# Batch 0's convolutions issued behind the score reductions of heads 6 to 8, and the conv weights loaded first by ScalarE's queue

## The chip, the cores and the metric

The kernel runs on one core of a Trainium2 chip. The metric is the device time of one execution in microseconds; the kernel before has a median of 501.28 us in 3 runs (501.0 to 501.86).

## What is computed

Four batches of eight attention heads (sequence 576, head size 64) are followed by a gated layer and by a gated layer with spatial mixing. Cut to what matters:

```python
cum = np.cumsum(np.maximum(s, 0.0), axis=-1)
scores = q @ k.T / 8 + np.minimum(-(cum[:, None] - cum[None, :]), 0.0)   # per head, causal
x = softmax(scores) @ v                      # heads laid side by side: 4 x 576 x 512
gate = sigmoid(sum(conv_w[k] * x_padded[:, k:k + S] for k in range(5)))  # causal, per channel
y = gate * (x @ w_val) @ w_out
h = np.maximum(y @ w_in, 0.0)                # 1024 wide: u, v
v_n = (v - mean(v)) / np.sqrt(var(v) + 1e-6)
out = (u * (w_spatial @ v_n + b_spatial)) @ w_out2
```

## The kernel before

A head's scores are made in five row tiles (64 rows and four of 128). TensorE writes them to two PSUM banks; VectorE's reduction in L253 adds the mask and takes the extreme of a row, then a read of one column puts it into `nm`; ScalarE makes the exponentials (L258), and their sums stand in `sm`. The function `transposes` turns the probabilities on TensorE (`pst`) and copies them on ScalarE (L301, tile `pt`). For each pair of heads `pv` multiplies them with v (`pso`, `psq`), and VectorE multiplies with the divisors R, which come back by DMA in a broadcast form, and writes x (L326 to L329). The first eight heads' scores are products of raw float32 data (L242); from head 8 on q and k are split on VectorE into a high and a low part (L100, `qk`, `kd`) and two products are summed (L244, L245). Wherever a weight is multiplied, `three` makes three products of high and low parts.

`conv(b, p)` is the convolution of one pair of heads (128 channels): ScalarE's scaling by the last tap (L338), four VectorE steps on 128x575, 574, 573 and 572 elements (L341), ScalarE's Tanh (L343). It needs x of the pair and `cw`, the conv weights.

The weights come as 64-bit floats. `from_f64` loads one (L402), unpacks it on ScalarE (L404), VectorE (L405 to L407) and GpSimd (L410, L411) into 32 bits; `fold_prep` and `weight_prep` then split it. `first_steps` does so for the conv weights, w_out (`wo_h`, `wo_l`), one half of w_in (`wih`, `wil`) and w_val, and then makes four folds, products of w_in and w_out (`psm` in the rows below, 12 products each); the result is `wch`, `wcl`.

The main loop over `w` issues scores of head w, transposes of head w - 1 and `pv` and `conv` of an earlier pair. In between, `more(n)` lets the weight steps and, from w = 9 on, the mixing layers (generators in `queue`) go on by a quota. A scheduler that simulates the program's time sets each engine's order; `tc.issue_after(X)` keeps what is issued in it behind X on X's own engine. `paced` uses it to keep the first weight steps behind `LAST["V"]`, the latest reduction issued. With `chain[0]`, from w = 18 to 31, TensorE keeps the order in which the code issues its work; this is so both in the kernel before and in the changed one.

## Time and profile before

| | |
|---|---|
| median of 3 runs | 501.28 us |
| the profiled execution's own time | 502.31 us |
| its span, first to last instruction | 500.5 us |
| mean granted clock of TensorE | 0.993 of full speed |
| TensorE busy with products | 474.9 us |
| VectorE busy | 320.2 us |
| ScalarE busy | 315.4 us |
| GpSimd busy | 165.8 us |

The rows further down are of this one execution. PE is TensorE, DVE VectorE, ACT ScalarE, POOL GpSimd, SPq the DMA issues of SyncE. Times are microseconds from the span's start. A line such as L341 is that of the kernel before; L75 and L100 are helpers which many steps share, so there the tiles tell the steps apart. A busy share is a mean over stages which different engines set, so the stretches are read one by one.

### The profile page before, as it was taken

The page shows a single profiled execution, that of the slowest core. Times are in us where ns is not written, and L with a number is a line of the kernel's source. Part 1 is how long each engine was busy: PE and PEld are TensorE (multiplying, and loading weights), DVE is VectorE, ACT ScalarE, POOL GpSimd, SP SyncE. Part 2 cuts the span into 40 slices and gives each one's busy share as a digit, 9 for nine tenths or more (in the row PEclk, how much of TensorE's full clock was granted, in tenths as well). Part 3 has the DMA queues.
Part 4 walks back from the last instruction along what each step waited for, and adds up shares of the span by engine and source line. Part 5 has one row for each costly group of instructions (what it writes and reads, how often), then busy time and mean ns, then how long its engine had stood idle before and what let it go on. Part 6 is the DMA issues. An engine that isn't in the chain of part 4 may idle for free.

```text
span 500.5 us, 9139 instructions
## 1 busy us (share of the span) xinstructions
PE 474.9 (95%) x3138; PEld 400.7 (80%) x3138; DVE 320.2 (64%) x835; ACT 315.4 (63%) x796; POOL 165.8 (33%) x183
## 2 busy tenths in 40 slices
PE   8697789979999999999999999999999999999997
PEld 5453457768777898998879999888778989988997
DVE  5599999698989885655578476555794453124120
ACT  2787968786776876675577758674876624234322
POOL 5587452045583103103243023012342022136130
PEclk9898999999999999999999999999999999999999
DMA  3876477558383644287531412784510072600002
GB/s 93 223 250 209 108 256 252 158 158 236 118 265 113 182 128 123 76 252 231 145 88 43 130 47 80 230 249 129 168 42 28 0 279 54 211 1 2 0 13 84
DMA packets 51567, 68.23 MB, mean 136 GB/s; under 512 B 23936, under 2 KB 39456, under 8 KB 51520
## 3 DMA queue, kind: packets, MB, share of 16 engines
q1 hardware_dynamic: 46592, 62.84, 42.3%
q10 hardware_dynamic: 4928, 4.80, 2.9%
q8 instruction: 25, 0.41, 0.4%
q14 instruction: 22, 0.18, 0.1%
HBM read 54.91 MB, written 9.16 MB: 128 GB/s over the span
## 4 chain that ended last, share of the span: by engine, by line
PE 63%; DVE 20%; DMA 7%; ACT 3%; issue 3%; POOL 2%; SPq 1%; DVEq 0%; ACTq 0%; POOLq 0%
PE psm L75 45%; PE pso L75 5%; PE pst L75 5%; DVE p L253 4%; DVE z L341 3%; DMA wv<-wv_d 2%; PE pss L244 2%; DMA raw<-in_qk 2%; PE pss L245 2%; DVE v L583 2%; PE psw L75 1%; DVE qk L100 1%; DVE wg L407 1%; ACT p L258 1%; PE pss L242 1%
## 5 line engine op out<-in xcount | busy, mean ns | idle before, releaser
L258 ACT ACTIVATE p<-p,nm 64x64 f32<-64x64 f32 (+4 forms) x160 | 88.5, 554 | 22.6 <-DVE nm L253 22.2
L253 DVE CUSTOM_DVE_ANT_0 p<-pss,mask 64x64 f32<-64x64 f32 (+4 forms) x160 | 62.7, 412 | 25.1 <-PE pss L245 17.7
L301 ACT ACTIVATE pt<-pst 128x512 f32<-128x512 f32 (+2 forms) x128 | 59.0, 495 | 28.3 <-PE pst L75 28.1
L341 DVE SCALAR_TENSOR_TENSOR z<-x,cw,z 128x575 f32<-128x575 f32 (+1 forms) x64 | 57.3, 896 | 7.4 <-ACT z L338 7.1
L75 PE MATMUL pst<-ident,p 128*128 128x128 f32 x416 | 60.1, 276 | 2.0 <-ACT p L258 1.8
L100 POOL TENSOR_TENSOR y<-gt,y 128x288 fp32r<-128x288 f32 x32 | 27.1, 847 | 102.8 <-ACT y L93 102.8
L100 POOL TENSOR_TENSOR g<-gt,g 128x288 fp32r<-128x288 f32 x32 | 28.8, 903 | 95.0 <-ACT g L93 94.7
L75 PEld LDWEIGHTS pst<-ident,p 128*128 128x128 f32 x416 | 48.4, 141 | 11.2 <-ACT p L258 4.3
L75 PE MATMUL psm<-g,wch 128*128 128x288 f32 x256 | 55.1, 299 | 1.2 <-DVE wcl L100 0.9
L75 PE MATMUL pso<-pt,vraw 128*64 128x512 f32 (+4 forms) x320 | 52.1, 448 | 0.0
L75 PE MATMUL psm<-wch,g 128*128 128x512 f32 x144 | 47.7, 400 | 0.0
L244 PE MATMUL pss<-qk 128*64 128x64 f32 (+1 forms) x144 | 43.6, 320 | 2.7 <-DVE nm L253 2.3
L75 PEld LDWEIGHTS psm<-g,wch 128*128 128x128 f32 x256 | 42.4, 189 | 2.0 <-DVE wcl L100 1.2
L75 PE MATMUL psm<-y,wv 128*128 128x288 f32 x288 | 42.0, 297 | 0.5 <-ACT ot L629 0.5
L75 PE MATMUL psm<-xvh,wv 128*128 128x288 f32 x192 | 40.2, 300 | 1.7 <-DMA wv<-wv_d 1.3
L245 PE MATMUL pss<-kd,cn 66*64 66x64 f32 (+1 forms) x144 | 41.1, 294 | 0.0
L242 PE MATMUL pss<-raw 128*128 128x320 f32 (+4 forms) x96 | 31.5, 432 | 9.6 <-DVE nm L253 6.0
L75 PEld LDWEIGHTS psm<-y,wv 128*128 128x128 f32 x288 | 39.6, 188 | 0.9 <-ACT ot L629 0.7
L524 DVE TENSOR_TENSOR gt<-psm,u 128x288 f32<-128x288 f32 x32 | 14.5, 456 | 39.3 <-PE psm L75 31.2
L75 PEld LDWEIGHTS pso<-pt,vraw 128*64 128x64 f32 (+1 forms) x320 | 19.3, 138 | 23.4 <-issue 16.7
L75 PE MATMUL psm<-wsh,vh 128*128 128x288 f32 x128 | 38.0, 299 | 0.0
L75 PE MATMUL psm<-g,wcl 128*128 128x288 f32 x128 | 38.0, 297 | 0.0
(142 smaller groups left out, 1118.9 us busy)
## 6 DMA issues: line engine op xcount, KB each, us to landing
raw<-in_qk SPq DMA_DIRECT2D x24, 448.0 KB
wv<-wo_d SPq DMA_DIRECT2D x12, 512.0 KB
R<-r_d SPq DMA_DIRECT2D x32, 160.0 KB
wv<-wv_d SPq DMA_DIRECT2D x10, 512.0 KB
out<-ot ACTq DMA_DIRECT2D x32, 144.0 KB
vraw<-in_vp SPq DMA_DIRECT2D x32, 128.0 KB
cn<-qk SPq DMA_DIRECT2D x24, 144.0 KB
raw<-in_qk SPq DMA_DIRECT2D x48, 64.0 KB
```

The source lines that it names most:

```text
L75: m = op(*a, **k)
L100: eng.tensor_tensor(out=out_, in0=in_, in1=f(hi), op=ALU.subtract)
L242: nc.tensor.matmul(pst[0:m, o:o + b - a], r[:, 1, q0:q0 + m], r[:, 0, k0 + a:k0 + b], start=True, stop=True)
L244: nc.tensor.matmul(pst[0:m, o:o + b - a], qa[:, q0:q0 + m], kb[:, k0 + a:k0 + b], start=True, stop=False)
L245: nc.tensor.matmul(pst[0:m, o:o + b - a], qc[0:KD, q0:q0 + m], kd[0:KD, k0 + a:k0 + b], start=False, stop=True)
L253: LAST["V"] = V.tensor_tensor_reduce(out=row[:, a:b], in0=src, in1=mask[0:m, o:o + b - a], scale=-0.125, scalar=3.0e38 if a == 0 else nm[0 ...
L258: A.activation(row, row, AF.Exp, bias=nm[0:m, i:i + 1], scale=-1.0, accum_out=sm[h // 2 % 2][0:m, h % 2, i:i + 1])
L301: A.activation(PT[h][:, to:to + n], pt[:, o:o + n], AF.Copy)
L341: V.scalar_tensor_tensor(out=z[:, d:], in0=x[:, :S - d], scalar=cw[:, p, k:k + 1], in1=z[:, d:], op0=ALU.mult, op1=ALU.add)
L407: V.scalar_tensor_tensor(out=up, in0=a.bitcast(I32), scalar=3, in1=up, op0=ALU.logical_shift_left, op1=ALU.bitwise_or)
L524: V.tensor_tensor(out=t, in0=psrc, in1=other, op=ALU.mult)
L583: V.tensor_scalar(out=v[0:m], in0=v[0:m], scalar1=mv[0:m, 0:1], scalar2=rs[0:m], op0=ALU.subtract, op1=ALU.mult)
```

## The change

`from_f64` issues loads of fewer than 512 columns, which are the conv weights alone, on ScalarE's queue and the others on SyncE's as before. The conv weights are prepared right after the function's definition, ahead of all other weights and of `first_steps`. In the main loop, batch 0's convolutions leave their place behind `pv` at w = 2, 4, 6 and 8: pair 0 is issued behind the scores of head 6, pair 1 behind those of head 7, pairs 2 and 3 behind those of head 8, each behind the latest reduction. The last batch's last convolution stays at w = 32.

```diff
-        SY.dma_start(r, src.rearrange("p (c t) -> p c t", t=2))
+        (A if n < 512 else SY).dma_start(r, src.rearrange("p (c t) -> p c t", t=2))
...
+    cw = early.tile([128, NP, 5], F32, name="cw")
+    V.tensor_copy(cw, from_f64(conv_w, 20).rearrange("p (c k) -> p c k", k=5))
...
     def first_steps():
-        nonlocal cw
-        cw = early.tile([128, NP, 5], F32, name="cw")
-        V.tensor_copy(cw, from_f64(conv_w, 20).rearrange("p (c k) -> p c k", k=5))
...
+    LATER = {6: [0], 7: [1], 8: [2, 3]}
     prep(0)
     for w in range(NH + 1):
         chain[0] = 18 <= w < 32
...
         if w % 2 == 0 and (0 < w <= H or w == NH):
             pv(w - 2)
-            conv((w - 2) // H, ((w - 2) % H) // 2)
+            if w == NH:
+                conv(B - 1, NP - 1)
+        for p in LATER.get(w, []):
+            with tc.issue_after(LAST["V"].ins):
+                conv(0, p)
```

VectorE around the scores of head 4, before (`p_125` are the probabilities of even heads, `x_381` is x of pair 0, `z` the convolution's output):

```order
L268 RECIPROCAL rin<-den 128x10
L341 SCALAR_TENSOR_TENSOR z<-x_381,cw,z 128x575
L253 ISA p_125,nm<-pss,mask 128x448
L253 ISA nm 128x1
L100 TENSOR_TENSOR xvl_973<-x_381,xvh_972 128x576
L253 ISA p_125,nm<-pss,mask 128x256
L253 ISA nm 128x1
L341 SCALAR_TENSOR_TENSOR z<-x_381,cw,z 128x574
L100 TENSOR_TENSOR wil<-wg,wih 128x512
L341 SCALAR_TENSOR_TENSOR z<-x_381,cw,z 128x573
L253 ISA p_125,nm<-pss,mask,nm 128x320
```

The same place now:

```order
L268 RECIPROCAL rin<-den 128x10
L253 ISA p_125,nm<-pss,mask 128x448
L253 ISA nm 128x1
L100 TENSOR_TENSOR xvl_973<-x_381,xvh_972 128x576
L253 ISA p_125,nm<-pss,mask 128x256
L253 ISA nm 128x1
L253 ISA p_125,nm<-pss,mask,nm 128x320
```

The three conv steps have left this place, and one split of w_in that stood ahead of the last reduction stands behind it.

VectorE around the scores of head 7 (`p_128`, odd heads; `qk` and `kd_117` are the splits of head 8), before:

```order
L253 ISA p_128,nm<-pss,mask 128x448
L253 ISA nm 128x1
L100 TENSOR_TENSOR qk<-raw_66,qk 64x576
L407 SCALAR_TENSOR_TENSOR wg<-wg 128x512
L100 TENSOR_TENSOR kd_117<-raw_66,qk 64x576
L326 TENSOR_TENSOR x_724<-pso,R 128x384
L328 TENSOR_TENSOR x_724<-pso,R 128x128
L329 TENSOR_TENSOR x_724<-psq,R 128x64
L253 ISA p_128,nm<-pss,mask 128x256
L253 ISA nm 128x1
```

and now:

```order
L341 SCALAR_TENSOR_TENSOR z<-x_381,cw,z 128x574
L253 ISA p_128,nm<-pss,mask 128x448
L253 ISA nm 128x1
L407 SCALAR_TENSOR_TENSOR wg<-wg 128x512
L100 TENSOR_TENSOR wv<-wg,wv 128x512
L341 SCALAR_TENSOR_TENSOR z<-x_381,cw,z 128x573
L100 TENSOR_TENSOR qk<-raw_66,qk 64x576
L100 TENSOR_TENSOR kd_117<-raw_66,qk 64x576
L253 ISA p_128,nm<-pss,mask 128x256
L253 ISA nm 128x1
```

Two of pair 0's conv steps now stand ahead of head 7's 256-column reduction, and the x of pair 2 (`x_724`) has left the place ahead of it.

TensorE from head 7's 448-column product (`raw_67`) to head 8's first products (`qk`, `kd_117`), before; the rows left out are more fold products:

```order
L242 MATMUL pss<-raw_67 128x448
L75 MATMUL psm<-wih,wo_h 128x512
...
L75 MATMUL psm<-wil,wo_h 128x512
L242 MATMUL pss<-raw_67 128x256
L242 MATMUL pss<-raw_67 128x320
L75 MATMUL psm<-wih,wo_h 128x512
...
L75 MATMUL psm<-wil,wo_h 128x512
L244 MATMUL pss<-qk 64x64
L245 MATMUL pss<-kd_117,cn_115 64x64
L244 MATMUL pss<-qk 128x192
```

and now, from head 7's 256-column product on:

```order
L242 MATMUL pss<-raw_67 128x256
...
L75 MATMUL pst<-ident,p_125 128x128 x2
L242 MATMUL pss<-raw_67 128x320
L244 MATMUL pss<-qk 64x64
L75 MATMUL psm<-wih,wo_h 128x512
...
L75 MATMUL psm<-wil,wo_h 128x512
L245 MATMUL pss<-kd_117,cn_115 64x64
L244 MATMUL pss<-qk 128x192
```

Before, one fold stands ahead of head 7's last two products and one ahead of head 8. Now both stand, one behind the other, between the two products of head 8's first tile.

## Rows read from the trace of the kernel before

**Rows 1.** The page's first part: engine, busy time (share of the span), instructions.

```profile
PE 474.9 (95%) x3138; PEld 400.7 (80%) x3138; DVE 320.2 (64%) x835; ACT 315.4 (63%) x796; POOL 165.8 (33%) x183
```

**Rows 2.** Busy time by stretch: length, PE, PEld, DVE, ACT, POOL, clock, DMA, GB/s.

```profile
40.00:88.00 48.00, 40.52 (x203) 24.69 (x202) 47.07 (x122) 37.58 (x97) 23.68 (x16) 0.96 0.65 206
88.00:100.00 12.00, 12.00 (x81) 8.82 (x79) 7.22 (x22) 9.24 (x23) 0.00 (x0) 1.00 0.57 164
100.00:126.00 26.00, 23.03 (x164) 19.43 (x163) 24.14 (x63) 19.94 (x50) 13.99 (x12) 1.00 0.67 196
126.00:160.00 34.00, 32.89 (x173) 25.43 (x172) 32.05 (x75) 24.56 (x58) 21.19 (x21) 1.00 0.53 167
```

**Rows 3.** The chain of waits in order of time: start, length, work.

```profile
85.02 3.02 PE psm L75 x12
...
422.69 74.71 PE psm L75 x516
```

**Rows 4.** VectorE's timeline, 88 to 102: start, length, work, idle time ahead, its releaser.

```profile
91.91 0.22 DVE L253 CUSTOM_DVE_ANT_0 p<-pss,mask 64x64 f32<-64x64 f32 x1 [0.33 <-PE pss L245]
...
94.23 0.49 DVE L253 CUSTOM_DVE_ANT_0 p<-pss,mask 128x320 f32<-128x320 f32 x1 [1.82 <-PE pss L245]
...
96.50 0.69 DVE L100 TENSOR_TENSOR wil<-wa,wih 128x512 fp32r<-128x512 f32 x1 [1.77 <-PE pst L75]
...
99.48 0.56 DVE L326 TENSOR_TENSOR x<-pso,R 128x384 f32<-128x384 f32 x1 [0.81 <-DMA R<-r_d]
...
100.95 0.55 DVE L253 CUSTOM_DVE_ANT_0 p<-pss,mask,nm 128x320 f32<-128x320 f32 x1
```

**Rows 5.** The timeline of the start, all engines.

```profile
11.54 0.42 SPq L402 DMA_DIRECT2D wg<-in_conv_w  x1
...
12.01 0.45 SPq L402 DMA_DIRECT2D wg<-in_woT  x1
...
13.56 0.18 DVE L405 TENSOR_SCALAR wg<-wg 128x20 f32<-128x20 f32 x1 [1.42 <-ACT wg L404]
...
21.38 1.39 PE L242 MATMUL pss<-raw 128*64 128x64 f32 x4 [3.41 <-DMA raw<-in_qk]
```

**Rows 6.** Conv steps of L341 by stretch: length, busy (count), clock, DMA share, GB/s.

```profile
40.00:68.00 28.00, 7.25 (x8) 0.94 0.56 180
...
76.00:100.00 24.00, 3.23 (x4) 1.00 0.67 205
```

**Rows 7.** The timeline around heads 7 to 9, VectorE and TensorE.

```profile
71.76 0.35 DVE L253 CUSTOM_DVE_ANT_0 p<-pss,mask 128x192 f32<-128x192 f32 x1
...
79.59 0.19 PE L244 MATMUL pss<-qk 128*64 128x64 f32 x1
...
99.54 0.30 PE L244 MATMUL pss<-qk 128*128 128x320 f32 x1
```

**Rows 8.** TensorE's timeline, probabilities times v.

```profile
30.18 2.20 PE L75 MATMUL pso<-pt,vraw 128*64 128x512 f32 x16
...
44.70 3.84 PE L75 MATMUL pso<-pt,vraw 128*64 128x512 f32 x16
```

**Rows 9.** Busy time in the 4 us ahead and in those of the second product.

```profile
40.00:44.00 4.00, 2.32 (x10) 0.99 (x8) 4.00 (x14) 3.46 (x10) 2.26 (x2) 1.00 0.70 238
44.00:48.00 4.00, 3.51 (x13) 1.24 (x13) 4.00 (x10) 3.16 (x9) 3.46 (x2) 0.62 0.72 236
```

**Rows 10.** The timeline of GpSimd and VectorE around two conv steps.

```profile
58.15 1.04 POOL L411 TENSOR_TENSOR wa<-wr 128x512 int32<-128x512 int32 x1 [3.07 <-DVE nm L253]
...
58.60 1.20 DVE L341 SCALAR_TENSOR_TENSOR z<-x,cw,z 128x575 f32<-128x575 f32 x1
...
61.48 0.80 DVE L341 SCALAR_TENSOR_TENSOR z<-x,cw,z 128x574 f32<-128x574 f32 x1
```

**Rows 11.** VectorE's timeline, the first split of head 8.

```profile
75.78 0.76 DVE L100 TENSOR_TENSOR qk<-raw,qk 64x576 fp32r<-64x576 f32 x1
```

More of the change, by code (lines that the diff above doesn't have):

```diff
@@ L634, in tile_stickbreak_attention_moe @@
     queue = []
-    cw = None
     def more(n):
```

## The prediction

> **What bounds the kernel now.** I read the busy line of the page first: TensorE 474.9 us of a span of 500.5, VectorE 320.2 [rows 1]. That is an average over stages, so the second view is busy time by stretch [rows 2]. In it TensorE idles 7.48 us between 40 and 88 us (48 less 40.52), nothing between 88 and 100, 2.97 between 100 and 126 and 1.11 between 126 and 160. VectorE is the mirror image: it idles 0.93 us in 40 to 88, 4.78 in 88 to 100 and 1.86 in 100 to 126. So VectorE sets the pace of heads 4 to 7, TensorE that of heads 8 and 9 with their folds, VectorE again that of heads 10 and 11. The chain of waits ends in one TensorE piece of 74.71 us [rows 3]: late in the kernel the end moves only by what TensorE no longer loses early on. From head 23 on the two orders of TensorE are the same row for row.
>
> The four waits that make up VectorE's idle time after 88 us are 0.33, 1.82, 1.77 and 0.81 us; the first three end on TensorE, the last on the DMA of the divisors R for pair 3 [rows 4]. There is room there for VectorE work, and no room for it between 40 and 88.
>
> **The conv weights, first and by ScalarE's queue.** Three small VectorE steps, about 0.18 us each, now stand between the load of s and the end of the running sum: 3 x 0.18 = 0.54 us later for the sum and the row of it that head 0 needs [rows 5]. SyncE's list loses one issue, which held it from 11.54 to 12.01: 0.47 us sooner for what stands behind, the load of head 2 among it. VectorE's wait of 1.42 us for ScalarE's step on these weights goes, but TensorE then still waits 3.41 us for head 2's load until 21.38, so what head 1 gains ends there. The load of head 2 moves by 0.54 - 0.47 = 0.07 us. I take 0, between 0.5 lost (the delay reaches head 0's first product whole) and 0.5 gained (only the SyncE issue counts). ScalarE's table load now stands behind one DMA issue and has no one waiting for it until the running sum is done.
>
> **The convolutions of batch 0.** Before, the eight VectorE steps of pairs 0 and 1 take 7.25 us between 40 and 68, in the stretch that VectorE paces; pair 2's four take 3.23 us between 76 and 100 [rows 6]. Now pair 0's stand behind head 6, pair 1's behind head 7, pairs 2 and 3 behind head 8. The tie to the last reduction binds VectorE to its own order, so no other engine waits for a new semaphore; ScalarE's first conv step stays where it was in its list, its Tanh moves back with VectorE's steps, and what reads the gate is far behind. Nothing is added or dropped: at the last reduction of head 11 both VectorE lists have done the same work. The gain can therefore be no more than VectorE idle time, and after 40 us that is 0.93 + 4.78 + 1.86 = 7.57 us.
>
> Step one, to head 8. In the new TensorE order both folds (12 products each) stand behind head 8's first product, and that needs the PSUM bank which head 7's 256-column reduction frees. Up to that reduction the new VectorE list holds, against the old list up to head 7's 192-column reduction, five conv steps fewer (5 x 0.91 = 4.5 us, 0.91 being 7.25 / 8) and in their place three reductions, the two splits of head 8 and one more weight step, about 4.2 us. So it is reached 0.3 us before the old row's end at 72.1, at 71.8. Two folds at 3.02 us [rows 3] are done at 77.9. Before, they and head 7 were done at 79.6, where head 8's first product stood [rows 7]: 1.7 us gained.
>
> Step two, to the end of head 9. TensorE has 19.9 us of rows from there to head 9's last product at 99.54 [rows 7]; the new list holds no more, so it is there by about 97.6. Its reduction then ends some 0.6 us later, at 98.2, where it ended at 101.5 before [rows 4], because the wait for R and two weight steps no longer stand ahead of it: 3.3 us gained. TensorE by itself shows less, 99.54 - 97.6 = 1.9, so I hold 1.9 as the lower end.
>
> Step three, heads 10 and 11, paced by VectorE. The new list is 1.2 us shorter at head 9's end (one conv step and one weight step fewer) and equal at head 11's, so 1.2 us of the 3.3 is paid back. Of the 1.86 us that VectorE idled here I take half as filled, 0.9 (bounds 0 and 1.86). Sum: 3.3 - 1.2 + 0.9 = 3.0 us. From there TensorE paces and the gain reaches the end.
>
> What could lie in between: with the conv steps late, the x tiles are kept longer; x of pair 0 is next written at head 11, far behind. SyncE's list now loads head 6 ahead of two of the four w_val loads, so no head waits longer for its data. The product of probabilities and v for heads 2 and 3 cost 3.84 us where the same 16 products for heads 0 and 1 cost 2.20 [rows 8]: the granted clock was 0.62 there, after four us in which TensorE was busy 2.32 [rows 9]. TensorE's order up to there is unchanged, so I leave that loss of 1.64 us in (0 gained; 1.64 if the clock stays up).
>
> The profiled run took 502.31 us, so the sum gives 502.31 - 3.0 = 499.3 for it; that run stands 1.03 above the median of 501.28, so against the median it is **498.3 us**. The likeliest case's own range is 496.5 to 500.0 (4.8 gained if all idle time of 88 to 100 is refilled; 1.3 if step two gives only 1.9, step three pays back 1.2 and 0.6 of the idle time is filled).
>
> **Rivals.** *Cheaper conv steps.* A conv step that meets a GpSimd row takes longer: 1.20 us at 58.60 with GpSimd busy from 58.15 to 59.19, 0.80 us at 61.48 without [rows 10]. GpSimd is idle from 88 to 100 [rows 2]. If the eight moved steps all fall to 0.80, that is 7.25 - 6.40 = 0.85 us more: 497.4. For it: pair 2's four steps, 3.23 us, were already there. Against it: most new places lie before 88, where GpSimd still works. [...]
>
> *Head 8 late (slower).* Head 8's first product now has 24 fold products queued behind it on TensorE. It needs head 8's data, whose split was done on VectorE at 75.78 + 0.76 = 76.54 [rows 11]. Before, the folds ran meanwhile. If that split comes no sooner than it did, the folds end at 76.54 + 6.04 = 82.6, 3.0 us later than 79.6, and less the 1.2 us by which VectorE's list is shorter at head 9's end the time is 501.28 + 3.0 - 1.2 = 503.1. It decides against me once head 8's first product starts later than 79.6 - 6.0 = 73.6 us. Against it: the load is released by head 6's last product, and VectorE's list up to head 6's end is shorter by the eight conv steps alone by 7.25 us.
>
> *Given back later.* Between heads 9 and 22 the lists of TensorE and VectorE differ too, and one more wait of 1 us there or two costs what VectorE gained: TensorE lost 1.11 us in 126 to 160 already. With 2.7 us lost, 501.0. This is also where I put the case that waits for loads, not VectorE, pace heads 4 to 7 (SyncE's list moves less than VectorE's).
>
> **How the numbers follow.** Forecast 0.60, cheaper steps 0.10, given back 0.14, head 8 late 0.16. The first two are faster: 0.70; the third is same: 0.14; the fourth slower: 0.16. About 0.2% (1.0 us) is what a measurement of this kernel can tell from no change. For 8 in 10 the range runs from 496.0, with some 0.07 below it (all bounds on the good side), to 502.6, with some 0.11 of the slow case above it.
>
> **What would show it.** Right: VectorE full from 40 us on with its idle time of 88 to 100 us mostly gone; head 8's first product at 71 to 73 us; head 9's last reduction ending near 98; TensorE's idle time in 40 to 88 down from 7.5 to about 5.5 us; the piece that ends the chain as long as before and 3 us sooner. Wrong: head 8's first product after 73.6 with TensorE idle ahead of it; head 0's first product more than 0.5 us later; the gain there at 100 us and gone by 230.

## The result, and the profile after

| | before | after |
|---|---|---|
| median | 501.19 us (500.02 to 501.86, 6 runs) | 506.29 us (504.63 to 509.93, 6 runs) |
| the profiled execution's own time | 502.31 us | 505.85 us |
| its span | 500.5 us | 504.1 us |
| mean granted clock of TensorE | 0.993 | 0.983 |

The ratio is 1.010 (95% interval 1.0064 to 1.0137): the changed kernel is about 5 us slower, where 3 us faster was forecast. The two profiled executions, from which the rows come, are 3.5 us apart (505.85 less 502.31), so they show some 70% of it. Helper lines keep their numbers; L506, L522, L575 and L583 of before are L509, L525, L578 and L586 now.

The busy line of the page of after (us, share of the span, instructions), to be read against [rows 1]:

```profile
PE 479.0 (95%) x3138; PEld 403.9 (80%) x3138; DVE 324.8 (64%) x835; ACT 315.5 (63%) x796; POOL 164.2 (33%) x183
```

The counts of instructions are the same. TensorE is busy 4.1 us longer (474.9 before) and idle 25.1 us, 0.5 less than before (504.1 less 479.0; 500.5 less 474.9). The mean granted clock is lower too (0.983 against 0.993), so the first question is where the clock was low. Busy time by stretch of after (columns: PE, PEld, DVE, ACT, POOL with counts, granted clock, DMA share, GB/s), against [rows 2]:

```profile
40.00:88.00 48.00, 41.78 (x219) 24.96 (x218) 44.95 (x118) 38.53 (x98) 23.71 (x16) 0.96 0.70 218
88.00:100.00 12.00, 9.96 (x60) 7.83 (x60) 10.33 (x31) 9.59 (x24) 0.00 (x0) 0.99 0.47 124
100.00:126.00 26.00, 25.71 (x172) 22.27 (x172) 25.11 (x59) 19.83 (x51) 13.68 (x13) 0.94 0.63 196
126.00:160.00 34.00, 31.74 (x160) 24.20 (x159) 30.36 (x70) 22.93 (x56) 18.87 (x20) 0.95 0.50 164
```

VectorE's idle time of 88 to 100 us fell from 4.78 to 1.67 us, as meant; that of 40 to 88 rose from 0.93 to 3.05. TensorE's idle time of 126 to 160 rose from 1.11 to 2.26 us, and the clock there is 0.95. TensorE's waits from 90 to 232 us, summed by what was waited for (us in total, times, longest), first before, then after:

```profile
PE pss L244 <- DVE nm L253: 1.9, 2, 1.2
PE psr L75 <- DVE rin L268: 1.0, 1, 1.0
PE psm L75 <- DMA wv<-wv_d: 1.0, 1, 1.0
PE psm L75 <- DVE wcl L100: 0.9, 1, 0.9
PE pst L75 <- ACT p L258: 0.7, 1, 0.7
PE psm L75 <- DVE gt L522: 0.4, 1, 0.4
```

```profile
PE psm L75 <- DMA wv<-wo_d: 2.2, 1, 2.2
PE psr L75 <- DVE rin L268: 2.1, 1, 2.1
PE psm L75 <- DVE wcl L100: 1.3, 1, 1.3
PE pss L244 <- DVE nm L253: 0.8, 2, 0.6
PE psm L75 <- DVE gt L525: 0.3, 1, 0.3
```

The sums differ by 0.8 us only (5.9 and 6.7; TensorE's whole idle time there is 5.96 and 7.02). But the longest wait of before is 1.2 us, and after has two of over two. What follows them differs. Rows of TensorE's timeline of after (start, us, engine, line, operation, tiles, and in brackets the idle time ahead with what ended it):

```profile
72.89 0.21 PE L244 MATMUL pss<-qk 128*64 128x64 f32 x1 [1.93 <-DVE nm L253]
...
96.51 0.39 PE L244 MATMUL pss<-qk 128*128 128x320 f32 x1
...
98.98 0.54 PE L75 MATMUL psm<-xvh,wv 128*128 128x288 f32 x2 [1.33 <-DVE wcl L100]
...
131.78 0.27 PE L75 MATMUL psr<-ident,rin 128*10 128x128 f32 x1 [2.14 <-DVE rin L268]
...
219.36 4.90 PE L75 MATMUL psm<-y,wv 128*128 128x288 f32 x24 [2.19 <-DMA wv<-wo_d]
```

Behind three of these pauses the granted clock goes to half (0.50 of full speed). Windows of 2 us of after, same columns as the stretches above:

```profile
100.00:102.00 2.00, 2.00 (x10) 2.00 (x10) 1.97 (x3) 2.00 (x5) 0.00 (x0) 0.50 0.17 36
...
134.00:136.00 2.00, 2.00 (x6) 1.51 (x5) 2.00 (x6) 2.00 (x7) 0.20 (x1) 0.50 0.02 4
136.00:138.00 2.00, 2.00 (x8) 1.58 (x7) 1.94 (x6) 1.81 (x4) 0.77 (x3) 0.67 0.79 287
...
220.00:222.00 2.00, 2.00 (x10) 2.00 (x10) 0.00 (x0) 0.00 (x0) 0.00 (x0) 0.50 0.88 244
222.00:224.00 2.00, 2.00 (x15) 2.00 (x14) 0.00 (x0) 0.41 (x1) 0.00 (x0) 0.84 0.53 165
```

As an estimate, a window at clock c loses its busy time times (1 - c). Summed over all 2-us windows that is 8.0 us in after and 3.0 in before. Behind 90 us it is 1.6 (98 to 104), 1.7 (132 to 138) and 1.4 (218 to 224), 4.8 in all, and nothing in before: there the clock falls twice, at 20 to 26 us (1.4) and at 44 to 50 (1.6, of which [rows 9] shows the start), and so it does in after (1.6 and 1.7). So the two spans compare like this:

| us | span | idle | lost to the clock | all other work |
|---|---|---|---|---|
| before | 500.5 | 25.6 | 3.0 | 471.9 |
| after | 504.1 | 25.1 | 8.0 | 470.9 |

By this account the clock is the whole difference of the pair: 5.0 us lost, 1.5 gained elsewhere. It is an account of one execution of each. The fall at 98 to 104 us did not move head 13's first reduction (141.76 us in after, and in changed_again, which has no fall there), so the sum alone does not give the time: the kernel w_out2_early below loses 7.8 us to the clock in a span of 501.6. The counts of products agree with the estimate: in 4 us with the clock at 0.57 the kernel pause_8 makes 19 where pause_4 makes 32 at 1.00, 0.59 of them (both rows stand below).

The path of the gain can be followed at the first reduction of a head, VectorE's L253 on 64x64 (heads whose place in the order is the same in both):

| head | 2 | 4 | 8 | 9 | 10 | 11 | 13 | 23 | 31 |
|---|---|---|---|---|---|---|---|---|---|
| before, us | 22.80 | 40.42 | 82.65 | 91.91 | 101.42 | 116.56 | 143.39 | 283.80 | 380.49 |
| after, us | 21.89 | 39.94 | 81.69 | 90.78 | 99.32 | 115.54 | 141.76 | 286.69 | 383.07 |

After is ahead by 0.5 to 2.1 us up to head 13 and 2.9 behind at head 23, which is the prediction's own sign of being wrong (the gain there at 100 us and gone by 230). The loss lies between 143 and 284 us for these rows: the scores of head 13 still come when VectorE is ready for them, and TensorE's lost time shows only where it has become the bound. TensorE's own idle time in 125 to 232 us rose by 1.7 us (2.99 to 4.69) and its clock loss there by 3.1 (1.7 and 1.4), 4.8 in all, against the 4.5 that the table shows between heads 13 and 23.

### The profile page after: what moved, and what is told of

It is laid out like the page before. It is cut to its first block, busy times and chain, and to the rows that moved or that the text cites. A ratio compares the mean times of both kernels' runs of the same rounds, so it can differ in the third digit from the quotient of the medians.

```text
span 504.1 us, 9153 instructions
## 1 busy us (share of the span) xinstructions
PE 479.0 (95%) x3138; PEld 403.9 (80%) x3138; DVE 324.8 (64%) x835; ACT 315.5 (63%) x796; POOL 164.2 (33%) x183
## 4 chain that ended last, share of the span: by engine, by line
PE 74%; DVE 15%; DMA 5%; POOL 2%; issue 1%; ACT 1%; SPq 0%; DVEq 0%; POOLq 0%; ACTq 0%
PE psm L75 52%; PE pso L75 7%; PE pst L75 6%; DVE p L253 3%; PE pss L244 3%; PE pss L245 3%; DVE z L341 3%; PE pss L242 2%; DMA out<-ot 1%; DMA raw<-in_qk 1%; DMA wv<-wo_d 1%; DVE qk L100 1%; DVE wg L407 1%; DVE kd L100 1%; DVE wr L407 1%
## 5 line engine op out<-in xcount | busy, mean ns | idle before, releaser
L253 DVE CUSTOM_DVE_ANT_0 p<-pss,mask 64x64 f32<-64x64 f32 (+4 forms) x160 | 62.7, 412 | 20.1 <-PE pss L245 13.1
L341 DVE SCALAR_TENSOR_TENSOR z<-x,cw,z 128x575 f32<-128x575 f32 (+1 forms) x64 | 58.5, 915 | 6.1 <-ACT z L338 5.7
L75 PE MATMUL psm<-y,wv 128*128 128x288 f32 x288 | 43.8, 305 | 2.7 <-DMA wv<-wo_d 2.2
L75 PEld LDWEIGHTS psm<-y,wv 128*128 128x128 f32 x288 | 40.9, 195 | 3.5 <-ACT p L258 2.3
L525 DVE SCALAR_TENSOR_TENSOR gt<-z,psm 128x288 f32<-128x288 f32 x32 | 14.3, 450 | 43.1 <-PE psm L75 40.4
```

The costliest lines, as they stand in the source:

```text
L75: m = op(*a, **k)
L253: LAST["V"] = V.tensor_tensor_reduce(out=row[:, a:b], in0=src, in1=mask[0:m, o:o + b - a], scale=-0.125, scalar=3.0e38 if a == 0 else nm[0 ...
L341: V.scalar_tensor_tensor(out=z[:, d:], in0=x[:, :S - d], scalar=cw[:, p, k:k + 1], in1=z[:, d:], op0=ALU.mult, op1=ALU.add)
L525: V.scalar_tensor_tensor(out=t, in0=other, scalar=more, in1=psrc, op0=ALU.add, op1=ALU.mult)
```

## The experiments

All ratios are against the kernel before on the same chip, with 95% intervals. "The falls" are stretches at the low clock. Theory A in the expectations is that the moved convolutions make the loss: they shift the order of heads 9 to 22, TensorE pauses at three new places, and the granted clock falls behind each (0.50 in the windows of after).

### Which part of the change it is

The conv weights alone (the change without its convolutions), for which Theory A gave 500.2 to 501.5 us and a mean granted clock of about 0.993:

```diff
-    LATER = {6: [0], 7: [1], 8: [2, 3]}
...
-            if w == NH:
-                conv(B - 1, NP - 1)
-        for p in LATER.get(w, []):
-            with tc.issue_after(LAST["V"].ins):
-                conv(0, p)
+            conv((w - 2) // H, ((w - 2) % H) // 2)
```

> One part alone: the conv weights are loaded first, by ScalarE's queue; the convolutions keep their old places. TensorE's order is then row for row that of the kernel before. [...] Rival B (the early weights make the loss): 504 us or more.

Measured: 501.98 us, ratio 1.0001 (0.9973 to 1.0028). The weights part is worth nothing measurable, as the prediction took it.

The convolutions alone (the kernel before with the `LATER` block; the weights stay in `first_steps` on SyncE's queue). The lines are against the changed kernel:

```diff
-        (A if n < 512 else SY).dma_start(r, src.rearrange("p (c t) -> p c t", t=2))
+        SY.dma_start(r, src.rearrange("p (c t) -> p c t", t=2))
...
-    cw = early.tile([128, NP, 5], F32, name="cw")
-    V.tensor_copy(cw, from_f64(conv_w, 20).rearrange("p (c k) -> p c k", k=5))
...
     def first_steps():
+        nonlocal cw
+        cw = early.tile([128, NP, 5], F32, name="cw")
+        V.tensor_copy(cw, from_f64(conv_w, 20).rearrange("p (c k) -> p c k", k=5))
```

> The other part alone: batch 0's convolutions behind heads 6, 7 and 8, the conv weights prepared where they were before and by SyncE's queue. TensorE's order is then row for row that of the changed kernel. Theory A: 505 to 508 us, a mean granted clock of 0.98 to 0.986, and the pauses near 98, 130 and 217 us with low clock behind them again. Rival B: within 1 us of the kernel before, 500.5 to 502.

Measured: 505.91 us, 1.0082 (1.0054 to 1.011). The moved convolutions are the loss. In its profile (span 504.5 us) the same places pause: 2.52 us ahead of head 8's first product, 1.33 at 99.41, 1.90 at 132.23 and 2.31 at 219.94, each with a fall behind it; 6.7 us lost to the clock in all.

The changed kernel once more, unaltered, on another chip:

> The changed kernel once more, as the reference for the next kernel on the same chip. 505.5 to 507 us, with TensorE waiting about 2.2 us for the w_out2 load near 217 us and low clock behind it.

Measured: 506.56 us (503.95 to 508.05), 1.0095 (1.0064 to 1.0126). The profiled execution was the fastest of its ten, 503.95 us. Its pauses are as long (2.79 at 131.91, 2.26 at 219.46), but no fall stands behind the one at 219. Windows of 2 us of this run, columns as above:

```profile
218.00:220.00 2.00, 0.54 (x4) 0.57 (x5) 0.78 (x2) 0.40 (x2) 0.00 (x0) 1.00 1.06 394
220.00:222.00 2.00, 2.00 (x17) 2.00 (x16) 0.00 (x0) 0.41 (x1) 0.00 (x0) 1.00 0.96 278
```

In 220 to 222 it made 17 products where after made 10. With the same order of heads it took 73.09 us from head 18's first reduction to head 23's, after 74.22: one fall is worth 1.1 us here. So a pause of a given length is not always followed by a fall, and part of the scatter of this kernel is whether it is.

### What a pause costs

Here the kernel before gets a chain of small VectorE steps late in its last batch, for which one tiny product waits, with TensorE's order held there. N is 4, 6, 8 and 16.

```diff
+                if b == 3 and hf == 0 and mc == 1:
+                    pz = early.tile([128, 6], F32, tag="bs", name="pz", bufs=2)[:, 0:1]
+                    V.tensor_copy(pz, pt[:, 0:1])
+                    for _ in range(N):
+                        V.tensor_scalar_add(pz, pz, 1e-9)
+                    chain[0] = True
+                    T.matmul(pt[0:1, 400:401], pz, pz, start=True, stop=True)
+                if b == 3 and hf == 0 and mc == 2:
+                    chain[0] = False
```

> The same with 5 small steps on VectorE: TensorE should wait about 1.2 us, as at three places of the kernel before behind which the clock stayed up. Theory A: the clock stays up, the time is that of the kernel before plus 1.2: 503.2 us. If the clock falls here too, 504.7 us.

> Between the two shorter pauses in the kernel before: 7 small steps on VectorE in the chain. With 5 steps TensorE waited 1.00 us and the clock stayed up, with 9 it waited 2.70 us and the clock fell to half. The wait here should be 1.3 to 2.2 us, which is where the pauses of the changed kernel lie (1.33, 1.93, 2.14 and 2.19 us). If a wait of this length is enough for a fall: the kernel before plus the wait plus about 1.6 us, 505 us. If not: plus the wait alone, 503.3 us.

> As the longer pause, in the kernel before, with 9 small steps on VectorE where that had 17 (its 17 made TensorE wait 4.95 us, since other VectorE work came in between). The wait here should be about 2 us, as long as the two of the changed kernel. Theory A: the granted clock falls behind it and the time is that of the kernel before plus 2 plus about 1.5: 505.5 us. Rival C: plus 2 alone, 504 us.

> The disputed cost by itself, in the kernel before: near 440 us, in the piece where TensorE alone works without a stop, one product is made to wait for a chain of 17 small VectorE steps that begins when an earlier product ends; TensorE's order is otherwise the same row for row. At some 0.11 us a step the pause is about 2 us, with the way there and back 2.3. Theory A (a pause of this length makes the clock fall afterwards, as the three did in the changed kernel): the pause plus about 1.7 us, 505.0 to 505.5 us. Rival C: the pause alone, 503.5 us.

The waiting product in TensorE's timeline, for N = 4, 6, 8 and 16:

```profile
458.41 0.19 PE L75 MATMUL psm<-pz 128*1 128x1 f32 x2 [1.00 <-DVE pz L606]
```

```profile
459.54 0.19 PE L75 MATMUL psm<-pz 128*1 128x1 f32 x2 [1.38 <-DVE pz L606]
```

```profile
460.06 0.19 PE L75 MATMUL psm<-pz 128*1 128x1 f32 x2 [2.70 <-DVE pz L606]
```

```profile
466.28 0.19 PE L75 MATMUL psm<-pz 128*1 128x1 f32 x2 [4.95 <-DVE pz L606]
```

And the 4 us behind it (columns as above), N = 4 and N = 8:

```profile
460.00:464.00 4.00, 4.00 (x32) 4.00 (x32) 0.69 (x1) 2.26 (x5) 0.00 (x0) 1.00 0.00 0
```

```profile
460.00:464.00 4.00, 3.94 (x19) 3.91 (x20) 0.69 (x2) 1.83 (x4) 0.00 (x0) 0.57 0.01 4
```

| N | pause in the profile | fall behind it | time, ratio |
|---|---|---|---|
| 4 | 1.00 us | no | 502.17, 1.0023 (0.9995 to 1.0051) |
| 6 | 1.38 us | no | 503.79, 1.0032 (1.0008 to 1.0056) |
| 8 | 2.70 us | yes, 0.57 (460 to 464) | 505.13, 1.0079 (1.0051 to 1.0106) |
| 16 | 4.95 us | yes, 0.59 (466 to 470) | 509.62, 1.0147 (1.0101 to 1.0194) |

The 0.11 us a step and the 0.3 us for the way there and back, expected for N = 16, are estimates that no run shows: from N = 4 to 6 the pause grew by 0.38 us, 0.19 a step. Where TensorE paces, the short pauses cost about their length (0.23% is 1.2 us, with nothing still inside its interval; 0.32% is 1.6), and the two longer ones cost the low clock too. From N = 6 to 8 the pause grows by 1.3 us and the time by 0.47%, 2.4 us; against the 1.1 us between them the window of N = 8 loses 1.7 (3.94 x 0.43), and the intervals are wide enough for either. These profiles have falls of their own in the rows of the kernel before: pause_8 one behind a wait of 1.62 us at 99.58, pause_16 one behind 1.02 us at 102.10, where before waits 1.20 us at 101.56 with no fall.

### Tries at one pause by other orders

Each of these kernels goes at one pause by moving something near it.

Eighteen transposes of a constant put ahead of the product that waits at 217, so that TensorE is not idle; they add work:

```diff
+                if b == 0 and mc == 2 and hf == 0:
+                    for _ in range(18):
+                        T.transpose(pt[:, 384:512], ident[:, 0:128], ident[:, 0:128])
```

> The changed kernel with 18 transposes of the identity (into columns of the PSUM bank that nothing reads) put ahead of the product of batch 0 that waited 2.19 us for its w_out2 load at 217 us, so that TensorE works through that wait. The wait for the load itself stays, and one group of 24 products now stands ahead of two score products, which I price at nothing. Theory A: the clock stays up behind 219 us and the time falls by the 1.7 us that the low clock cost there: about 504.6 us. Rival C (the waits themselves are the loss, the clock is beside the point): as the changed kernel or up to 1 us above it, 506.3 to 507.3 us.

Measured: 507.73 us, 1.010 (1.0059 to 1.0141). The transposes ran earlier than the wait, which stayed at 1.30 us. The profiled execution took 503.67 us at clock 0.997, with one fall, behind 2.35 us of waiting at 129.67; executions of the same kernel at 0.983 took 505.9 us of span and more. So it says nothing on the pause itself, but in it the clock and the time go together with one and the same code.

TensorE's order held from head 14 on instead of 18:

```diff
-        chain[0] = 18 <= w < 32
+        chain[0] = 14 <= w < 32
```

> The changed kernel with TensorE's order taken from the code from head 14 on, not from head 18. Up to TensorE's place behind head 13's 448-column product the order is that of the changed kernel; from there, two groups of 12 products and three score products stand ahead of the transpose of the divisors, on which TensorE waited 2.14 us at 129.6 to 131.8. Theory A (pauses of about 2 us and the low clock behind them are the loss): that pause and the fall behind it go, so at head 14 the changed kernel's loss turns back into its gain, and the time falls by 1.1 (pause beyond that of before) plus 1.7 (clock): 503.5 us where the wait for w_out2 near 217 us stays with its fall, about 501 us if it goes too. Rival D (the convolutions' new places cost in themselves, the clock is chance): 505.5 to 506.5 us.

Measured: 507.98 us, 1.0146 (1.0117 to 1.0175), no faster than the changed kernel (1.010 and 1.0095; the intervals just touch). The wait for the divisors is 2.43 us at 133.93 with a fall, and one of 2.31 at 73.15 has a fall too. With this order TensorE no longer waits for w_out2 at 217, but four waits of 0.7 to 1.3 us that after doesn't have came between 140 and 232.

The last convolution ahead of the divisors of pair 5 issued behind their reciprocal, on which the transposed divisors (`psr`) wait at 131:

```diff
-        V.reciprocal(out=R[p], in_=d)
+        LAST["N"] = V.reciprocal(out=R[p], in_=d)
...
-            conv((w - 3) // H, ((w - 3) % H) // 2)
+            if w != 11:
+                conv((w - 3) // H, ((w - 3) % H) // 2)
...
+            if w == 11:
+                with tc.issue_after(LAST["N"].ins):
+                    conv((w - 3) // H, ((w - 3) % H) // 2)
```

> The changed kernel with one thing more: the next batch's first convolution (heads 8 and 9) is issued behind the divisors of heads 10 and 11, so that VectorE makes these two small steps ahead of two conv steps (1.58 and 0.82 us in the changed kernel) and not behind them. Up to there the orders are those of the changed kernel; TensorE's rows from there to the start of batch 1's mixing come out anew. Theory A: TensorE's pause at 130 us shrinks from 2.14 us to under 0.7, the clock stays up behind it, and 1.5 + 1.7 us come back: 503 us, if the new rows behind hold no pause of 2 us; 505 if one does. Rival D (the convolutions' places cost in themselves): 506 us.

Measured: 508.3 us, 1.0121 (1.0092 to 1.015). The wait for the divisors shrank to 0.91 us at 133.73, but 1.66 us came back at 135.67 in another wait, with a fall behind the two; another at 73.57 (1.95 us) now had one too, and a third fall, at 94 to 100, stands behind 0.58 us.

The load of w_out2's third chunk in batch 0 by GpSimd's queue, in case SyncE's list held it back:

```diff
...
-        SY.dma_start(f(w), src[mc].rearrange("p t (k m) -> p t k m", k=4))
+        (G if src is wo_d and b == 0 and mc == 2 else SY).dma_start(f(w), src[mc].rearrange("p t (k m) -> p t k m", k=4))
...
```

> The changed kernel with one load moved from SyncE's queue to GpSimd's: the third quarter of w_out2 for batch 0, for which TensorE waited 2.19 us at 217 to 219.4 us. SyncE issued it at 213.55, behind a load of q and k that waited for its buffer from 211.0 to 212.6; the buffer that it fills was free at about 211.2. GpSimd has nothing else to do there. TensorE's order stays but for one pair of score products that moves by 12 products. Theory A (pauses of 2 us and the low clock behind them are the loss): the pause and the fall go, 2.2 + 1.7 us less than the changed kernel: 502.5 us, and head 23 that much sooner. If the fall is chance and costs nothing: 504.3 us. If the wait is taken up by another one behind it: as the changed kernel, 506.3 us.

Measured: 507.74 us, 1.0115 (1.0072 to 1.0159). The pause stays (2.15 us at 222.23), and the timeline says why: GpSimd itself waits 3.38 us for TensorE before it may issue, since the buffer is still being read. A row of GpSimd's timeline of this run:

```profile
215.49 0.79 POOL L509 DMA_DIRECT2D wv<-wo_d  x1 [3.38 <-PE psm L75]
```

The chain of waits of after shows the same load (start, length): 5.67 us from issue to landing, with less TensorE work than that left in the other buffer.

```profile
213.55 5.67 DMA wv<-wo_d
```

### Other places for the convolutions

Each convolution of pairs 0 to 2 one head earlier:

```diff
-    LATER = {6: [0], 7: [1], 8: [2, 3]}
+    LATER = {5: [0], 6: [1], 7: [2], 8: [3]}
```

> The changed kernel with every convolution of batch 0 one head earlier: pairs 0 to 3 behind heads 5, 6, 7 and 8. The orders of heads 9 to 22 come out anew. Rival D (the later the convolutions, the dearer): between the two kernels, 503 to 505 us. Theory A: it goes by the pauses of TensorE behind 126 us alone, 501 us without one of 2 us and 1.7 to 3 us more for each one.

Measured: 503.41 us, 1.0037 (1.0013 to 1.006). In the profile no pause over 0.3 us is left at 131, that at 218 is 1.51 us with no fall, and behind 90 us one fall remains, behind 1.22 us at 102; 4.9 us lost to the clock in all (8.0 in after).

Only pairs 2 and 3 moved:

```diff
-    LATER = {6: [0], 7: [1], 8: [2, 3]}
+    LATER = {2: [0], 4: [1], 8: [2, 3]}
```

> Half of the move: pairs 0 and 1 stay behind heads 2 and 4, pairs 2 and 3 go behind head 8, as in the changed kernel. TensorE's order is that of the kernel before up to its row 127, behind head 8's first products, so head 8's first product doesn't stand ahead of two folds here and the pause of 1.9 to 2.5 us ahead of it is not made. Theory A: 501 to 502 us if no pause of 2 us comes up behind 90 us, 1.7 to 3 us more for each that does. Rival D: the gain or loss of this half is in proportion to the steps moved, half of the loss: 504 us.

Measured: 507.28 us, 1.0117 (1.0078 to 1.0156). Its profile has two pauses in a row at 133 to 135 us (0.95 and 1.19) with a fall behind them, but only 4.5 us lost to the clock in all. "All other work" is 475.7 us where every kernel here without made pauses or added transposes has 469.4 to 471.9. The excess lies ahead of head 23. These 4 us have no explanation in the rows that were read; the account by pauses and falls doesn't cover this run.

### The pause at 217 taken away by another buffer

The third and fourth chunk of w_out2 of batch 0 are loaded into the tiles `wr`, which the weight steps no longer need then. The load need not wait for the buffer pair that TensorE reads.

```diff
         key = src is wo_d, b, mc
+        if src is wo_d and b == 0 and mc in (2, 3):
+            w = mid.tile([128, 1024], I32, tag="wr", name="wr", bufs=2)
+            w = w.bitcast(F32R).rearrange("p (t k m) -> p t k m", t=2, k=4)
+            SY.dma_start(f(w), src[mc].rearrange("p t (k m) -> p t k m", k=4))
+            return w[:, 0], w[:, 1]
         return AHEAD.pop(key) if key in AHEAD else load_chunk(src, mc)
```

In the changed kernel:

> The changed kernel; for batch 0 the third and fourth quarter of w_out2 are loaded into the two buffers in which the 64-bit weights were unpacked (idle by then) and no longer into the two buffers that the first two quarters use. TensorE's order stays except for nine rows at the place. Theory A: the wait of 2.2 us at 217 to 219 us goes, and with it the fall that stood behind it in two of three profiles of this order (1.1 to 1.7 us): 506.5 less 2.2 to 3.6, 503 to 504.3 us. If the wait is only passed on to batch 1's first loads: 506 us or more.

In the kernel before:

> The same two buffers in the kernel before. TensorE's 0.96 us wait at 224 us for a load of w_val goes, since that load's buffers come free sooner; the rows of heads 18 to 22 come out anew in part (63 of TensorE's). Theory A: 0 to 1 us faster than the kernel before, 500.6 to 501.6 us, if no pause of 2 us comes up in the new rows.

With the convolutions of one_head_earlier:

> Batch 0's convolutions one head earlier than in the changed kernel (behind heads 5, 6, 7, 8), the conv weights first, and w_out2's third and fourth quarter for batch 0 in the idle unpack buffers; three of TensorE's rows move against the kernel without the prefetch, which took 503.4 us. Theory A: its wait of 1.51 us goes, no fall stood behind it: 501.5 to 502 us, level with the kernel before. Rival D (the moved convolutions cost in themselves): 503 us or more.

With the weights part alone:

> The conv weights first by ScalarE's queue, the convolutions in their old places, and the same prefetch. The prefetch alone took 500.1 us where the kernel before took 501.2, the weights alone changed nothing that could be told. 499.8 to 500.5 us.

| kernel | with the early load | without it |
|---|---|---|
| changed | 503.30, 1.0027 (1.0003 to 1.005) | 506.56, 1.0095 |
| one head earlier | 500.79, 0.999 (0.9968 to 1.0012) | 503.41, 1.0037 |
| weights alone | 501.74, 1.0009 (0.9986 to 1.0031) | 501.98, 1.0001 |
| before | 500.07, 0.9978 (0.9956 to 1.0) | 1 |

Each ratio is against the kernel before on the run's own chip. TensorE's three longest waits from 90 to 232 us (us in total, times, longest; the others are 0.5 us or less), first of the changed kernel with the early load, then of the one with the convolutions a head earlier:

```profile
PE psr L75 <- DVE rin L268: 2.0, 1, 2.0
PE psm L75 <- DVE wcl L100: 0.9, 1, 0.9
PE pss L244 <- DVE nm L253: 0.6, 1, 0.6
```

```profile
PE pss L244 <- DVE nm L253: 1.0, 2, 0.6
PE psm L75 <- POOL y L100: 0.9, 1, 0.9
PE psm L75 <- ACT xvh L93: 0.5, 1, 0.5
```

With the pause at 217 gone the changed kernel gets back 0.68% (3.4 us), where the same edit is worth 0.22% (1.1 us) to the kernel before; the other 2.3 us are the pause that the change had brought and what followed it. What is left in it is the wait for the divisors at 133 with its fall, the one at 72 with a fall, and a fall at 92 to 98 behind 0.58 us. The kernel that has none of the three long pauses still has all of batch 0's convolutions late, one head less so, and is level with the kernel before: late convolutions as such cost nothing that can be told. That it beats the weights alone with the same early load (500.79 against 501.74, on the same chip) lies within the two intervals. The early load in the kernel before is the fastest version found, by 0.2%, which its interval just allows to be nothing.

### The falls at 21 and 44 us

The weights part with 24 transposes of a constant ahead of head 2's scores, where TensorE waits over 3 us, to see whether the early falls that both kernels have (20 to 26 and 44 to 50 us) are cheap to remove:

```diff
+                    if h == 2 and i == 0:
+                        for _ in range(24):
+                            with tc.issue_after(LAST["S"]):
+                                LAST["S"] = nc.tensor.transpose(pst[:, 384:512], ident[:, 0:128], ident[:, 0:128]).ins
...
```

> The conv weights first by ScalarE's queue, the convolutions in their old places, and 24 transposes of the identity (into PSUM columns that nothing reads) between head 1's last product and head 2's first, where TensorE waits 3.4 to 4.0 us for head 2's load and the clock is low for some 4 us afterwards in most of the profiles. They work for about 3 us of the wait. The orders from there to head 15 come out anew. Theory A: the clock stays up at 20 to 25 us, which gives 1 to 2 us if nothing later takes it back: 500 to 501 us. Rival C: 502 us or more.

Measured: 502.0 us, 1.0007 (0.998 to 1.0034). TensorE made 21 products in 18 to 20 us, where before has none, and the clock stayed at 1.00 up to 26. The falls only went to other places, 26 to 30 and 56 to 62 us, with 3.2 us lost to the clock where before loses 3.0. So the run doesn't show what these falls cost.

## Why the prediction was wrong, point by point

**The start: right.** 0 within 0.5 us was forecast for the conv weights; alone they measured 1.0001.

**Step one, to head 8: right in kind, blind to its pause.** Head 8's first product was forecast for 71 to 73 us and stands at 72.89; TensorE is through the folds behind it at 78.54, forecast 77.9, before 79.59 [rows 7], so 1.05 us are gained of 1.7. The rival "Head 8 late" put its point at 73.6, so it did not decide. What the step didn't name is the 1.93 us that TensorE idles ahead of that product, the whole wait for head 7's reductions now that no fold stands ahead of it. No fall stands behind it in after, changed_again and hold_217, and one does in convs_only, chain_from_14, divisors_first, w_out2_by_gpsimd and w_out2_early.

**Step two, to head 9: direction right, size off.** TensorE issues head 9's last product at 96.51 (forecast 97.6; the forecast's own sum, 77.9 + 19.9, gives 97.8). Its reduction was to follow 0.6 us later, but VectorE was at other rows. VectorE's timeline of after:

```profile
89.58 0.55 DVE L253 CUSTOM_DVE_ANT_0 p<-pss,mask,nm 128x320 f32<-128x320 f32 x1 [2.72 <-PE pss L245]
...
96.93 0.80 DVE L341 SCALAR_TENSOR_TENSOR z<-x,cw,z 128x572 f32<-128x572 f32 x1
97.65 0.68 DVE L100 TENSOR_TENSOR wil<-wa,wih 128x512 fp32r<-128x512 f32 x1
98.25 0.67 DVE L100 TENSOR_TENSOR wcl<-psm,wch 128x512 fp32r<-128x512 f32 x1
98.86 0.53 DVE L253 CUSTOM_DVE_ANT_0 p<-pss,mask,nm 128x320 f32<-128x320 f32 x1
```

VectorE waits 2.72 us for a product of head 8, which stands behind a fold on TensorE, and what it could not do then comes later. The reduction ends at 98.86 + 0.53 = 99.39, 2.1 us before the old 101.50 [rows 4], not 3.3; 0.5 to 0.9 of the 2.1 was there already at heads 2 and 4. A conv step and two weight steps fill VectorE's new room just ahead of the reduction, and `wcl` among them is what TensorE waits 1.33 us for at 98.98. Room that is filled by list order is not all gain: the filler can stand ahead of what others need.

**Step three, heads 10 and 11: about as forecast in kind.** Head 11's last reduction starts at 125.13 and ends at 125.66, where it ended at 126.68 before (row below): 1.0 us is left of the 3.0.

**"From there TensorE paces and the gain reaches the end": the step that failed.** TensorE does pace behind 126 us, but the gain doesn't reach the end. It loses 4.8 us to the low clock behind 90 us, where before loses nothing there, and 1.7 us more idle time in 125 to 232. The prediction's sum holds the clock as it was before and has no term for a fall behind a new wait. One place where the gain is held up is the wait for the divisors. In both kernels the same 611 products stand ahead of it. After reaches it at 129.64 us (131.78 less 2.14), before at 131.43; but the reciprocal starts at 131.51, before at 132.21. So TensorE comes 1.8 us sooner, VectorE only 0.7, and the pause is 1.1 us longer. The product that waits is still 0.7 us ahead of the old one (131.78 for 132.46); then the fall takes 1.7. Rows of TensorE, VectorE and GpSimd of before:

```profile
132.46 0.28 PE L75 MATMUL psr<-ident,rin 128*10 128x128 f32 x1 [1.03 <-DVE rin L268]
```

```profile
126.14 0.54 DVE L253 CUSTOM_DVE_ANT_0 p<-pss,mask,nm 128x320 f32<-128x320 f32 x1
...
128.53 0.75 DVE L100 TENSOR_TENSOR kd<-raw,qk 64x576 fp32r<-64x576 f32 x1
129.21 1.43 DVE L341 SCALAR_TENSOR_TENSOR z<-x,cw,z 128x575 f32<-128x575 f32 x1
130.56 1.00 DVE L266 TENSOR_SCALAR den<-sm 128x10 f32<-128x10 f32 x1
...
132.21 0.20 DVE L268 RECIPROCAL rin<-den 128x10 f32<-128x10 f32 x1
```

```profile
128.82 1.20 POOL L100 TENSOR_TENSOR g<-gt,g 128x288 fp32r<-128x288 f32 x1
129.98 1.55 POOL L411 TENSOR_TENSOR wa<-wr 128x512 int32<-128x512 int32 x1
```

Rows of after on VectorE, and on GpSimd at the same time:

```profile
127.87 1.37 DVE L100 TENSOR_TENSOR kd<-raw,qk 64x576 fp32r<-64x576 f32 x1
129.16 1.58 DVE L341 SCALAR_TENSOR_TENSOR z<-x,cw,z 128x575 f32<-128x575 f32 x1
130.67 0.15 DVE L266 TENSOR_SCALAR den<-sm 128x10 f32<-128x10 f32 x1
...
131.51 0.21 DVE L268 RECIPROCAL rin<-den 128x10 f32<-128x10 f32 x1
```

```profile
127.61 1.01 POOL L100 TENSOR_TENSOR g<-gt,g 128x288 fp32r<-128x288 f32 x1
128.58 1.55 POOL L411 TENSOR_TENSOR wa<-wr 128x512 int32<-128x512 int32 x1
```

The split took 1.37 us where the same one at 93.85, with GpSimd idle, took 0.74, and the conv step 1.58 where those of 88 to 100 us took 0.80. GpSimd was busy from 127.61 to 128.62 and from 128.58 to 130.13, so both ran beside its rows. But before has such meetings here too (GpSimd busy from 128.82 to 131.53): its conv step took 1.43 us, and the small row `den` ahead of the reciprocal 1.00, which is 0.15 in after. From the end of head 11's last reduction to the reciprocal VectorE takes 5.85 us in after and 5.53 in before, so the meetings explain 0.3 us of the longer pause at most.

The wait for w_out2 at 217 is new: before has none there, only 0.96 us for a load of w_val at 224.65. The order of the mixing products had changed: between the issue of this load and its use TensorE had 4.8 us of other work in before (210.09 to 214.87) and 3.6 in after (213.55 to 217.17), where the load took 5.67 us. That the pauses and what follows them are the loss is shown by the early load (3.4 us back) and by early_and_w_out2_early (level with before). How much the pause at 131 costs by itself is not shown: divisors_first and chain_from_14, which went at it, moved the wait elsewhere or kept it.

**"Given back later": the right mechanism, mis-sized.** The rival named one or two more waits of a microsecond between heads 9 and 22, 2.7 us and 501.0. The waits came there: 1.33 us at 99, the divisors' 1.1 us longer than before, and 2.19 us for w_out2. But TensorE's idle time in 90 to 232 us rose by 1.1 us only (5.96 to 7.02); three falls, at 1.4 to 1.7 us each, made 4.8. The prediction held the fall at 44 us [rows 8, 9] constant and did not carry its price over to the new waits. With the 3.1 us of clock behind 125 us (1.7 + 1.4) in its price the rival would have stood at 504.1, outside the range that was given.

**"Cheaper conv steps": seen, and paid for elsewhere.** The eight conv steps that now run in 76 to 100 us take 0.80 each (6.36 us by the windows of L341), as the rival had it, against 0.91 in [rows 6]. But other rows take longer. The second splits of k (`kd`, 24 rows) take 20.9 us in all where they took 17.8, all conv steps together 58.5 us against 57.3, and VectorE 324.8 against 320.2 with the same 835 instructions. That GpSimd's rows now meet these is argued from rows such as those at 127 to 131 us and was not tested.

**What stays open.** Why the same pause of about 2.2 us at 219 has a fall behind it in one execution and not in another; why some waits of 1 us or less have one; the 4 us of pairs_2_3_only; and how much of the loss each of the three places carries, since any edit near them also gave the products of heads 9 to 22 another order.

## What to carry to other kernels

Work moved off a paced stretch is only half a prediction: where TensorE paces further on, list its waits there (for a VectorE row, for a load into a buffer that it still reads itself), ask which rows ahead of each will move, and by how much less than TensorE itself. Give each wait that is new or grows a price for the low clock behind it (1.4 to 1.7 us here) with a chance, since it may come or not. Compare a row that looks slow with the same row of the kernel before, not with the fastest of its kind. Work moved into free room on one engine can make rows overlap with another engine's (here a conv step took 1.58 us beside GpSimd rows and 0.80 with GpSimd idle), so the other rows of both belong in the sum. The load that waited for a buffer that the consumer still read was mended here by another buffer (3.4 us back) and not by another queue.

## What was not expected of the hardware

- Pauses of 1.00 and 1.38 us in a busy TensorE left the granted clock at 1.0; those of 2.70 and 4.95 us were followed by a lower one (0.57 and 0.59 over the 4 us behind them). In the kernels with long pauses, falls stood behind most pauses of 1.9 us and more, and not behind 2.26 us in changed_again or 1.93 us at 73 in after. Some shorter ones had one too: 1.33 us at 99, 1.22 and 1.02 us at 102, and 0.58 us at 93 in three kernels (w_out2_early, w_out2_by_gpsimd, divisors_first). So the length of a pause alone did not decide here.
- One kernel's runs scatter with the mean granted clock: hold_217 took 503.67 us at 0.997 and 508.06 at 0.983, the changed kernel 504.63 at 0.986 and 509.93 at 0.976.
- Here a fall cost time where TensorE paced and not where VectorE did: that at 98 to 104 us (1.6 us of clock) leaves head 13 as far ahead in after as in changed_again (141.76 in both), which had no fall there. w_out2_early has three falls behind 70 us and 7.8 us lost to the clock in all, as much as after (8.0), and its profiled execution is 2.4 us shorter (503.43 against 505.85).
